# A recurrent attention layer with a gated feed-forward: loads and emission order rewritten, some steps moved to VectorE

## The chip, the cores and the metric

The kernel runs on one core of a Trainium2 chip. The metric is the device time of one execution in microseconds (us); of several executions the median is taken. A profile shows one execution: its span is the time from the first to the last instruction of the program. The engines are TensorE (PE, with its weight loads as PEld), VectorE (DVE), ScalarE (ACT), GpSimd (POOL) and SyncE (SP); SP issues most DMA transfers, POOL the weights' ones. Each engine works its own queue in order.

## The reference

Four sequences of 768 tokens, 8 heads of 48 channels. Per head a 48 x 48 state runs along the tokens:

```python
for t in range(S):
    cur = u * kt (outer) vt
    y[t] = rt @ (state + cur)
    state = wt * state + kt (outer) vt
```

The result, 3072 tokens of 384 channels, goes through a root-mean-square norm and a gated feed-forward of width 1536:

```python
xn  = x / sqrt(mean(x * x) + 1e-06) * rms_g
out = (silu(xn @ w_gate) * (xn @ w_val)) @ w_out
```

## The kernel before, in words

The tokens are cut into 24 chunks of 128, named n.j: n (0 to 5) is the place along the sequence, j (0 to 3) the sequence. Within a chunk the recurrence is written as matrix products. The steps of a chunk, each a small function of the program, are:

- load_w, load_r, load_k, load_v: DMAs on SP's queue, 192 KB each (384 KB for the w of n = 0 and 1, which are loaded together). The tiles rotate through 8 buffers each.
- ln and cs_mm: the logarithm of w (ScalarE) and its running sums on TensorE, in two PSUM banks (rings a and b, two banks each). For n = 0 and 1 both sums come from TensorE, later cs_add makes the second on VectorE. exp_r and exp_k (ScalarE) turn them into factors.
- r_mul, k_mul, w_tot: r and k times these factors, into bf16 tiles, and the decay of the chunk (VectorE; k_mul on POOL for the chunks listed in K_POOL).
- rk_pe and rk_tr: r and k transposed by TensorE and copied out of PSUM (n = 0 and 1), or transposed by a DMA (later).
- q_mm, q_mask_e, q_copy_o, q_mask_o: the products of r and k within the chunk, masked to the past.
- st_mm, st_new: the state after the chunk. cast_v: v in bf16.
- bonus_mul (POOL, two multiplications), bonus_sum (VectorE), bonus_v (POOL): the term with u.
- y_mm, x_add: the chunk's output x. x_sq, x_rstd, xn_mul: the norm; x_rstd takes two steps, on ScalarE for the chunks in RSTD_ACT, otherwise on POOL. xn_pe and xn_out (transposed by TensorE, copied out times the gain on VectorE), or xn_tr and xn_gain (by a DMA, and POOL) for n = 4 and 5.

Four chunks make a feed-forward group. Its 24 products of 512 columns, gate_mm.n.f and val_mm.n.f (f from 0 to 11, three matmuls each), use rings a and b too; silu (ScalarE) frees a bank of ring a and h_mul (VectorE) one of ring b. Then o_mm, o_out and out_dma give the output, 12 matmuls a chunk. The groups take chunks in order, except that chunks 0.0, 0.1, 1.0 and 1.1 make group 0 and 0.2, 0.3, 1.2 and 1.3 group 1. The weights of gate and val come in two parts: load_gv.0.x holds units 0 to 3, load_gv.1.x units 4 to 11 (x is 0 for gate, 1 for val). warm steps are matmuls of zeros whose result nobody reads.

What runs when is written out by hand: ORDER is a list of step names, and the program emits the steps in that order, so each engine's queue is the list with the other engines' steps taken out. All other PSUM tiles come from a ring of four banks, q. ScalarE holds one set of functions at a time: act (L234) emits a table load where a step needs the logarithm and exponential and the silu set is loaded, or the other way round.

Of the kernel before, what the change touches and what calls it, by code (L numbers as in the profile page):

```python
# [30 lines left out]
warm.1.0 warm.0.0 y_mm.0.1 load_k.1.1 load_r.1.1 load_k.0.3 load_v.0.3 q_mask_e.0.0 ln.0.3 w_tot.1.1 k_mul.1.0
r_mul.1.0 st_new.0.0 q_mask_o.0.0 w_tot.1.0 x_add.0.1 bonus_sum.0.0 rk_pe.1.0 rk_tr.1.0 k_mul.1.1 r_mul.1.1 st_mm.1.0
warm.4.0 cs_mm.0.3 x_sq.0.1 x_rstd.0.1 xn_mul.0.1 y_mm.0.0 bonus_v.0.0 q_mm.1.0 load_r.0.3 q_mask_e.1.0 x_add.0.0
q_mask_o.1.0 cs_mm.1.3 rk_pe.1.1 xn_pe.0.1 load_w.0.2 exp_k.0.3 warm.8.0 warm.7.0 warm.6.0 x_sq.0.0 exp_r.0.3
rk_tr.1.1 cast_v.0.3 ln.0.2 bonus_mul.1.1 k_mul.0.3 load_r.1.3 load_r.0.2 r_mul.0.3 xn_out.0.1 bonus_sum.1.0 warm.5.0
w_tot.0.3 st_new.1.0 bonus_sum.1.1 y_mm.1.0 rk_pe.0.3 rk_tr.0.3 x_rstd.0.0 bonus_v.1.0 st_mm.0.3 x_add.1.0 st_new.0.3
cs_mm.0.2 load_v.1.1 q_mm.0.3 warm.9.0 exp_r.0.2 q_copy_o.0.3 cast_v.1.1 xn_mul.0.0 exp_k.0.2 x_sq.1.0 load_v.0.2
x_rstd.1.0 exp_k.1.3 cast_v.0.2 xn_mul.1.0 exp_r.1.3 q_mm.1.1 q_mask_e.1.1 q_mask_o.1.1 r_mul.0.2 w_tot.0.2 load_k.0.2
bonus_v.1.1 load_gv.0.1 load_gv.0.0 warm.10.0 warm.11.0 st_mm.1.1 xn_pe.0.0 y_mm.1.1 st_new.1.1 x_add.1.1 cs_mm.1.2
x_sq.1.1 x_rstd.1.1 exp_r.1.2 q_mask_e.0.3 k_mul.0.2 st_mm.0.2 warm.14.0 warm.13.0 warm.12.0 xn_pe.1.0 load_k.1.3  # L40
load_gv.1.0 k_mul.1.3 q_mask_o.0.3 rk_pe.0.2 st_new.0.2 r_mul.1.3 xn_out.1.0 xn_out.0.0 xn_mul.1.1 load_r.1.2
load_k.1.2 load_v.1.3 bonus_mul.0.2 rk_pe.1.3 y_mm.0.3 xn_pe.1.1 xn_out.1.1 rk_tr.0.2 rk_tr.1.3 load_v.1.2 load_gv.1.1
q_mm.0.2 q_copy_o.0.2 warm.15.0 q_mm.1.3 load_w.2.1 load_w.2.0 q_mask_o.0.2 q_mask_e.0.2 w_tot.1.3 r_mul.1.2 exp_k.1.2
val_mm.0.1 val_mm.0.3 y_mm.0.2 bonus_sum.0.2 bonus_v.0.2 x_add.0.2 warm.19.0 q_copy_o.1.3 w_tot.1.2 q_mask_e.1.3
warm.18.0 warm.17.0 warm.16.0 gate_mm.0.3 gate_mm.0.1 q_mask_o.1.3 k_mul.1.2 x_sq.0.2 rk_pe.1.2 x_rstd.0.2 silu.0.3
silu.0.1 xn_mul.0.2 gate_mm.0.2 h_mul.0.3 warm.20.0 xn_pe.0.2 gate_mm.0.0 bonus_mul.1.2 bonus_mul.1.3 load_w.2.2
load_r.2.1 load_r.2.0 h_mul.0.1 silu.0.2 rk_tr.1.2 load_w.2.3 val_mm.0.2 val_mm.0.0 h_mul.0.2 bonus_sum.1.2
bonus_sum.1.3 bonus_mul.0.3 gate_mm.0.9 silu.0.9 silu.0.0 h_mul.0.0 bonus_sum.0.3 q_mm.1.2 gate_mm.0.6 silu.0.6
gate_mm.0.5 silu.0.5 q_copy_o.1.2 q_mask_e.1.2 load_wo.0.0 load_wo.2.0 bonus_v.0.3 gate_mm.0.7 gate_mm.0.4 load_wo.1.0
q_mask_o.1.2 bonus_v.1.3 bonus_v.1.2 val_mm.0.9 cast_v.1.3 x_add.0.3 xn_out.0.2 val_mm.0.5 x_sq.0.3 cast_v.1.2  # L50
h_mul.0.9 y_mm.1.3 h_mul.0.5 y_mm.1.2 x_add.1.3 load_k.2.1 x_add.1.2 silu.0.4 silu.0.7 val_mm.0.4 gate_mm.0.8 x_sq.1.3
x_rstd.0.3 x_sq.1.2 h_mul.0.4 x_rstd.1.3 silu.0.8 xn_mul.0.3 xn_mul.1.3 val_mm.0.8 val_mm.0.6 h_mul.0.8 h_mul.0.6
x_rstd.1.2 gate_mm.0.10 st_mm.1.2 st_new.1.2 gate_mm.0.11 xn_mul.1.2 xn_pe.1.3 xn_pe.1.2 val_mm.0.10 xn_pe.0.3
st_mm.1.3 silu.0.10 silu.0.11 load_r.2.2 h_mul.0.10 ln.2.1 val_mm.0.7 val_mm.0.11 xn_out.0.3 xn_out.1.2 h_mul.0.11
h_mul.0.7 cs_mm.2.1 load_k.2.0 load_r.2.3 ln.2.0 cs_mm.2.0 cs_add.2.1 exp_r.2.1 cs_add.2.0 xn_out.1.3 exp_r.2.0
exp_k.2.1 ln.2.2 w_tot.2.1 r_mul.2.1 o_mm.0.0 w_tot.2.0 k_mul.2.1 bonus_mul.2.1 ln.2.3 exp_k.2.0 r_mul.2.0 o_out.0.0
o_mm.0.1 cs_mm.2.2 cs_mm.2.3 cs_add.2.2 o_out.0.1 exp_r.2.2 w_tot.2.2 cs_add.2.3 exp_k.2.2 exp_k.2.3 exp_r.2.3
load_v.2.1 r_mul.2.2 w_tot.2.3 r_mul.2.3 load_k.2.3 o_mm.0.2 val_mm.1.6 gate_mm.1.6 k_mul.2.0 silu.1.6 val_mm.1.0
cast_v.2.1 gate_mm.1.0 st_mm.2.1 gate_mm.1.1 bonus_mul.2.0 o_out.0.2 h_mul.1.6 bonus_sum.2.1 silu.1.0 silu.1.1
val_mm.1.1 gate_mm.1.5 load_k.2.2 bonus_v.2.1 bonus_mul.2.3 k_mul.2.2 k_mul.2.3 out_dma.0.1 load_v.2.0 gate_mm.1.4  # L60
h_mul.1.0 st_new.2.1 st_new.1.3 h_mul.1.1 o_mm.0.3 silu.1.5 gate_mm.1.7 val_mm.1.4 rk_tr.2.1 rk_tr.2.0 bonus_sum.2.0
bonus_sum.2.3 o_out.0.3 q_mm.2.0 silu.1.4 h_mul.1.4 q_mask_e.2.1 silu.1.7 q_copy_o.2.1 gate_mm.1.3 val_mm.1.7
q_mask_e.2.0 q_copy_o.2.0 cast_v.2.0 load_v.2.3 load_v.2.2 load_w.3.1 out_dma.0.0 load_r.3.2 cast_v.2.2 rk_tr.2.3
rk_tr.2.2 out_dma.0.2 load_w.3.0 st_mm.2.0 st_mm.2.2 q_mask_o.2.1 val_mm.1.3 q_mask_o.2.0 bonus_v.2.0 load_v.3.2
load_w.3.3 y_mm.2.1 gate_mm.1.2 load_r.3.3 load_k.3.2 load_k.3.0 h_mul.1.7 y_mm.2.0 silu.1.3 silu.1.2 val_mm.1.5
gate_mm.1.8 load_w.3.2 load_r.3.0 load_r.3.1 gate_mm.1.9 bonus_mul.2.2 cast_v.2.3 st_new.2.2 st_new.2.0 x_add.2.0
x_add.2.1 q_mm.2.2 x_sq.2.0 h_mul.1.5 h_mul.1.3 val_mm.1.9 q_mask_e.2.2 bonus_sum.2.2 x_sq.2.1 silu.1.8 val_mm.1.2
load_k.3.1 gate_mm.1.11 q_copy_o.2.3 silu.1.9 x_rstd.2.1 x_rstd.2.0 h_mul.1.9 st_mm.2.3 gate_mm.1.10 q_copy_o.2.2
xn_mul.2.0 xn_mul.2.1 silu.1.11 bonus_v.2.2 q_mask_o.2.2 q_mask_o.2.3 bonus_v.2.3 xn_pe.2.0 val_mm.1.8 y_mm.2.2
h_mul.1.2 load_k.3.3 st_new.2.3 q_mask_e.2.3 silu.1.10 ln.3.0 xn_pe.2.1 val_mm.1.10 y_mm.2.3 h_mul.1.8 ln.3.1  # L70
val_mm.1.11 cs_mm.3.0 cs_mm.3.1 x_add.2.2 x_sq.2.2 h_mul.1.10 x_add.2.3 ln.3.3 x_sq.2.3 x_rstd.2.2 h_mul.1.11
xn_mul.2.2 o_mm.1.0 cs_add.3.1 xn_out.2.0 cs_add.3.0 o_out.1.0 exp_r.3.1 exp_r.3.0 xn_pe.2.2 o_mm.1.1 exp_k.3.0 ln.3.2
x_rstd.2.3 xn_mul.2.3 exp_k.3.1 k_mul.3.0 load_k.4.1 w_tot.3.0 w_tot.3.1 out_dma.0.3 load_v.3.1 out_dma.1.0 r_mul.3.0
r_mul.3.1 cast_v.3.2 cs_mm.3.2 xn_out.2.2 k_mul.3.1 cs_add.3.2 cs_mm.3.3 xn_pe.2.3 exp_k.3.2 cs_add.3.3 exp_r.3.3
o_out.1.1 rk_tr.3.0 k_mul.3.2 o_mm.1.2 xn_out.2.3 r_mul.3.3 st_mm.3.2 o_out.1.2 exp_k.3.3 w_tot.3.3 exp_r.3.2 o_mm.1.3
k_mul.3.3 rk_tr.3.1 o_out.1.3 load_v.3.0 load_v.3.3 w_tot.3.2 xn_out.2.1 st_new.3.2 r_mul.3.2 val_mm.2.5 q_mm.3.0
q_copy_o.3.0 gate_mm.2.0 q_mask_e.3.0 bonus_mul.3.0 gate_mm.2.5 cast_v.3.0 st_mm.3.0 val_mm.2.0 q_mask_o.3.0
cast_v.3.1 bonus_sum.3.0 q_mask_e.3.1 cast_v.3.3 bonus_v.3.0 st_mm.3.1 y_mm.3.0 silu.2.0 h_mul.2.0 load_k.5.3
bonus_mul.3.3 bonus_mul.3.1 silu.2.5 load_k.5.2 out_dma.1.2 x_add.3.0 h_mul.2.5 gate_mm.2.7 gate_mm.2.1 st_new.3.1
x_sq.3.0 silu.2.1 silu.2.7 val_mm.2.6 val_mm.2.1 gate_mm.2.6 h_mul.2.1 gate_mm.2.3 val_mm.2.7 load_w.4.1 rk_tr.3.2  # L80
rk_tr.3.3 load_k.4.0 load_k.4.3 load_r.4.2 load_w.4.0 load_v.4.0 load_r.4.1 out_dma.1.3 load_r.5.0 q_copy_o.3.1
load_r.4.3 load_r.4.0 st_new.3.0 silu.2.6 h_mul.2.6 gate_mm.2.2 x_rstd.3.0 q_mask_o.3.1 q_mm.3.2 bonus_sum.3.1
h_mul.2.7 val_mm.2.2 q_mask_e.3.3 q_mask_e.3.2 bonus_mul.3.2 silu.2.2 q_copy_o.3.2 gate_mm.2.4 val_mm.2.3 st_mm.3.3
bonus_v.3.1 y_mm.3.1 xn_mul.3.0 xn_pe.3.0 silu.2.4 silu.2.3 load_k.4.2 q_mask_o.3.2 gate_mm.2.11 h_mul.2.3 gate_mm.2.8
# [604 lines left out]
```

## Time and profile before

| | |
|---|---|
| time, median of 3 runs | 212.51 us |
| lowest and highest run | 207.11 and 213.64 us |
| span of the profiled execution | 202.6 us |
| time of the profiled execution itself | not given by its profile |
| busy: PE, DVE, ACT, POOL | 190.6, 146.2, 137.0, 135.1 us |
| DMA | 32.41 MB, mean 160 GB/s |
| first feed-forward product | 34.40 us after the start |

Line numbers such as L602 are those of the kernel before. In a row of a group stand the line, the engine, the operation, what it writes and reads, the shapes and the count; after the bar the busy time, the mean time of one in ns, and the idle time of the engine ahead of these instructions with what ended it. In a row in order of time the first two numbers are the start and the duration in us.

### The profile page before, as it was taken

To read this page: it belongs to the slowest core of one execution; us is meant where nothing else is said; L and a number is where in the kernel's file an instruction comes from. 1 tells how busy PE (TensorE), PEld (TensorE's weight loads), DVE (VectorE), ACT (ScalarE), POOL (GpSimd) and SP (SyncE) were. 2 spreads that over 40 slices of the span, in tenths; PEclk is the share of its full clock that TensorE was granted. 3 is DMA by queue.
4 is the path that set the end of the run, shared out by engine and by line. 5 is a ranking of instruction groups with operands and counts; after the bars stand their busy time and mean duration, and the time that the engine had idled before them with its cause. 6 is when DMAs were issued, how large, how long until landed. Compare 5 with 4: busy or idle time off the path is not lost.

```text
span 202.6 us, 4390 instructions
## 1 busy us (share of the span) xinstructions
PE 190.6 (94%) x1573; PEld 112.8 (56%) x1573; DVE 146.2 (72%) x289; ACT 137.0 (68%) x278; POOL 135.1 (67%) x198
## 2 busy tenths in 40 slices
PE   1998887899999999999999999999999999999994
...
DVE  6489787458786989998779889878688782075411
...
GB/s 165 232 235 168 245 177 206 203 191 192 217 191 220 195 148 190 209 216 197 220 173 221 231 188 228 186 199 131 38 135 123 52 22 80 57 0 42 39 134 101
DMA packets 121566, 32.41 MB, mean 160 GB/s; under 512 B 116420, under 2 KB 120392, under 8 KB 121544
## 3 DMA queue, kind: packets, MB, share of 16 engines
...
q14 instruction: 10, 0.08, 0.1%
...
## 4 chain that ended last, share of the span: by engine, by line
PE 59%; SPq 11%; DMA 9%; DVE 6%; POOL 5%; ACT 5%; issue 3%; DVEq 0%; POOLq 0%
PE ps_au L602 9%; SPq L249 9%; PE ps_bu L602 8%; PE ps_bv L602 8%; PE ps_av L602 8%; PE ps_qx L634 6%; PE ps_qv L634 5%; DMA rt<-in_r_dram 4%; PE ps_qu L634 3%; PE ps_qz L634 2%; DMA wt<-in_w_dram 2%; DMA vt<-in_v_dram 2%; DMA out_dram<-ob 2%; POOL ruk L457 1%; SPq L262 1%
## 5 line engine op out<-in xcount | busy, mean ns | idle before, releaser
L634 PEld LDWEIGHTS <-ht 128*128 128x128 bf16 x300 | 28.5, 98 | 17.3
L620 DVE TENSOR_TENSOR ht<-ps_bu,sg 128x512 bf16<-128x512 f32 x38 | 26.1, 687 | 14.5 <-PE ps_bu L602 9.8
L602 PEld LDWEIGHTS <-wg_sb 128*128 128x128 bf16 x216 | 23.2, 114 | 19.1 <-issue 0.6
L602 PEld LDWEIGHTS <-wv_sb 128*128 128x128 bf16 x216 | 22.9, 114 | 18.2
L236 ACT ACTIVATE sg<-ps_au 128x512 bf16<-128x512 f32 x38 | 22.6, 595 | 14.7 <-PE ps_au L602 13.8
L620 DVE TENSOR_TENSOR ht<-ps_bv,sg 128x512 bf16<-128x512 f32 x34 | 23.3, 686 | 12.7 <-ACT sg L236 6.4
L602 PE MATMUL ps_au<-xnt,wg_sb 128*128 128x512 bf16 x114 | 30.9, 380 | 0.4 <-ACT sg L236 0.4
L602 PE MATMUL ps_bu<-xnt,wv_sb 128*128 128x512 bf16 x114 | 30.9, 380 | 0.0
L236 ACT ACTIVATE sg<-ps_av 128x512 bf16<-128x512 f32 x34 | 20.2, 595 | 14.0 <-PE ps_av L602 12.9
L602 PE MATMUL ps_bv<-xnt,wv_sb 128*128 128x512 bf16 x102 | 27.6, 380 | 0.0
L602 PE MATMUL ps_av<-xnt,wg_sb 128*128 128x512 bf16 x102 | 27.6, 380 | 0.0
L457 POOL TENSOR_TENSOR ruk<-rt,kt 128x384 f32<-128x384 f32 x24 | 24.3, 1013 | 4.2 <-DMA kt<-in_k_dram 4.2
L451 POOL TENSOR_TENSOR rk<-kt,ek 128x384 bf16<-128x384 f32 x20 | 19.9, 1002 | 9.0 <-ACT ek L236 9.0
L458 POOL TENSOR_TENSOR ruk<-ruk,u_bc 128x384 f32<-128x384 f32 x24 | 24.0, 999 | 1.9
L467 POOL TENSOR_TENSOR ydiag<-vt,diag 128x384 f32<-128x384 f32 x24 | 20.1, 841 | 7.5 <-DVE diag L462 5.1
L550 ACT ACTIVATE junk<-xb 128x384 bf16<-128x384 f32 x24 | 12.5, 520 | 5.2 <-DVE xb L545 5.0
L634 PE MATMUL ps_qx<-wo_sb,ht 128*128 128x384 bf16 (+1 forms) x96 | 15.9, 316 | 0.0
L563 ACT ACTIVATE xn<-xb,rstd 128x384 bf16<-128x384 f32 x24 | 14.3, 610 | 0.7 <-POOL rstd L559 0.6
L510 POOL TENSOR_SCALAR_AFFINE_SELECT qts<-qts 128x512 bf16<-128x512 bf16 x20 | 12.5, 636 | 3.1 <-ACT qts L503 3.1
L234 ACT ACT_TABLE_LOAD x10 | 12.8, 1283 | 1.8 <-PEq L673 1.7
L462 DVE TENSOR_REDUCE diag<-ruk 128x8 f32<-128x384 f32 x24 | 12.9, 543 | 0.0
L634 PE MATMUL ps_qv<-wo_sb,ht 128*128 128x384 bf16 x72 | 12.7, 326 | 0.0
...
## 6 DMA issues: line engine op xcount, KB each, us to landing
...
wt<-in_w_dram SPq DMA_DIRECT2D x4, 384.0 KB, 4.3
wo_sb<-in_moe_w_out_dram POOLq DMA_DIRECT2D x3, 384.0 KB, 7.3
wg_sb<-in_moe_w_gate_dram POOLq DMA_DIRECT2D x1, 768.0 KB, 10.0
```

Of the source, the lines that this page charges most:

```text
L234: nc.scalar.preload_act_table_set(table_name)
L236: return nc.scalar.activation(**kw).ins
L249: dmas["load_" + which, n, j] = nc.sync.dma_start(out=inp[which, n, j], in_=t[j, :, n * L:(n + 1) * L, :].rearrange("h t d -> t h d")).ins
L451: eng.tensor_tensor(out=rk[:, n % 2, j, 1, :, 0:D], in0=inp["k", n, j], in1=bank["cs_k", n, j][:, 0:DM].rearrange("p (h d) -> p h d", h=H) ...
L457: nc.gpsimd.tensor_tensor(out=ruk[n, j], in0=inp["r", n, j], in1=inp["k", n, j], op=ALU.mult)
L458: nc.gpsimd.tensor_tensor(out=ruk[n, j], in0=ruk[n, j], in1=u_bc, op=ALU.mult)
L462: nc.vector.tensor_reduce(out=diag[n, j].rearrange("p h o -> p (h o)"), in_=ruk[n, j], axis=mybir.AxisListType.X, op=ALU.add)
L467: nc.gpsimd.tensor_tensor(out=ydiag[n, j], in0=inp["v", n, j], in1=diag[n, j].to_broadcast([128, H, D]), op=ALU.mult)
L563: nc.scalar.activation(out=xn, in_=xb[n, j], func=AF.Copy, scale=rstd[n, j][:, 1:2])
L602: nc.tensor.matmul(ps, lhsT=units(ws, c, f), rhs=xnt[n].rearrange("p (c x) -> p c x", c=KC)[:, c, :], start=(c == 0), stop=(c == KC - 1))
L620: nc.vector.tensor_tensor(out=ht[n][:, f, :], in0=bank.pop(("v", n, f)), in1=bank.pop(("sg", n, f)), op=ALU.mult)
L634: nc.tensor.matmul(ps[:, cols], lhsT=ht[n][:, f, b * L:(b + 1) * L], rhs=wo_sb[:, f, cols], start=(f == 0), stop=(f == FC - 1))
```

## The change

ORDER is replaced by another list of the same steps. In it the r and k of chunks 0.0, 1.0, 0.1 and 1.1 are loaded first behind the two w tiles, then v; load_gv.0.1 and load_gv.0.0 stand among the first group's attention steps; the attention of 0.2, 0.3, 1.2 and 1.3 stands mostly behind the first feed-forward products; six warm steps stand ahead of the first cs_mm and five behind the last o_mm.

The lists that give a step to an engine change as well: some casts of v and products of x with 1/rms go to VectorE, as do five copies of the transposed r and k, nine of POOL's k_mul and, the other way, five copies of outputs go from VectorE to ScalarE; x_rstd goes to ScalarE for eight more chunks.

```diff
-load_w.0.1 load_w.0.0 load_v.0.1 ln.0.1 load_r.0.1 load_k.0.1 load_k.0.0 load_r.0.0 cs_mm.0.1 ln.0.0 exp_k.0.1
...
+warm.6.0 load_w.0.0 ln.0.0 warm.15.0 load_w.0.1 warm.2.0 warm.18.0 load_r.0.0 load_k.0.0 load_k.1.0 warm.0.0 warm.13.0
+load_k.0.1 bonus_mul.0.0 load_r.1.0 ln.0.1 load_r.0.1 cs_mm.0.0 bonus_mul.0.1 exp_r.0.0 load_r.1.1 load_k.1.1
...
+exp_k.0.2 xn_out.1.0 xn_out.1.1 gate_mm.0.2 bonus_mul.0.3 exp_r.0.2 load_k.0.2 w_tot.0.2 load_v.0.3 rk_tr.0.3 q_mm.0.3
...
-    CAST_ACT = sel("00 01 02 03 10 11 12 13")
+    CAST_ACT = sel("00 10 11 20 50")
     EXPR_SB = sel("")
-    K_POOL = sel("02 03 12 13 20 21 22 23 30 31 32 33 40 41 42 43 50 51 52 53")
-    EXPK_SB = sel("10 11") | K_POOL
+    XN_DVE = sel("00 01 02 03 10 12 13 22 30 32 41 42 51 52 53")
+    CAST_DVE = sel("12 13 22 23 30 40 41 42 43 51 52")
+    K_POOL = sel("03 13 20 21 23 30 32 40 41 43 51")
+    EXPK_SB = sel("02 03 10 11 12 13 20 21 22 23 30 31 32 33 40 41 42 43 50 51 52 53")
...
-    RK_DVE = sel("")
+    RK_DVE = sel("00 02 03 10 13")
     ODD_DVE = sel("00 01 10 11")
-    RSTD_ACT = sel("00 01 10 11")
-    OUT_DVE = sel("00 02 10 12 20 22 30 32 40 42 50 52 53")
+    RSTD_ACT = sel("00 02 10 11 13 21 33 43 50 51 52 53")
+    OUT_DVE = sel("01 10 22 32 41 42 52 53")
...
         if (n, j) in CAST_ACT:
             nc.scalar.copy(out=vb[n, j], in_=inp["v", n, j])
+        elif (n, j) in CAST_DVE:
+            nc.vector.tensor_copy(out=vb[n, j], in_=inp["v", n, j])
         else:
             nc.gpsimd.tensor_copy(out=vb[n, j], in_=inp["v", n, j])
...
-        nc.scalar.activation(out=xn, in_=xb[n, j], func=AF.Copy, scale=rstd[n, j][:, 1:2])
+        if (n, j) in XN_DVE:
+            nc.vector.tensor_scalar(out=xn, in0=xb[n, j], scalar1=rstd[n, j][:, 1:2], scalar2=None, op0=ALU.mult)
+        else:
+            nc.scalar.activation(out=xn, in_=xb[n, j], func=AF.Copy, scale=rstd[n, j][:, 1:2])
```

200 lines of the change are left out of this document (99 added, 101 removed).

## The prediction

> **What bounds the kernel now.** I read the page's busy shares, its slices and its chain first, then the table by stretches of time.
>
> ```profile
> span 202.6 us, 4390 instructions
> PE 190.6 (94%) x1573; PEld 112.8 (56%) x1573; DVE 146.2 (72%) x289; ACT 137.0 (68%) x278; POOL 135.1 (67%) x198
> PE   1998887899999999999999999999999999999994
> DVE  6489787458786989998779889878688782075411
> PE 59%; SPq 11%; DMA 9%; DVE 6%; POOL 5%; ACT 5%; issue 3%; DVEq 0%; POOLq 0%
> ```
>
> ```profile
> 20.00:30.00 10.00, 8.47 (x97) 5.25 (x95) 8.08 (x19) 9.71 (x25) 7.62 (x9) 0.84 1.11 212
> 60.00:70.00 10.00, 10.00 (x65) 5.77 (x64) 7.32 (x16) 6.01 (x11) 8.65 (x10) 1.00 0.91 198
> 80.00:90.00 10.00, 10.00 (x103) 6.52 (x101) 9.57 (x21) 9.06 (x21) 6.49 (x11) 1.00 1.04 219
> ```
>
> There are two regimes. From about 40 us TensorE is full: 10.00 of 10 us, even where VectorE is busy 9.57 (columns: PE, PEld, DVE, ACT, POOL, clock, DMA share). Before that it is not (8.47 at a clock of 0.84 from 20 to 30 us): the first feed-forward product waits for four chunks (0.0, 0.1, 1.0, 1.1) to go through attention. So time changes in two ways only: the first product starts earlier or later, with more or less work left behind it, or another engine takes the bound later.
>
> **The start, now.** TensorE's and VectorE's order of time:
>
> ```profile
> 5.95 0.82 PE L396 MATMUL ps_au<-lw,mw 128*128 128x384 bf16 x2
> 11.88 0.34 PE L520 MATMUL ps_qz<-vb,rk 128*128 128x96 bf16 x4
> 12.06 0.49 PE L396 MATMUL ps_av<-lw,mw 128*128 128x384 bf16 x2
> 16.71 0.49 PE L396 MATMUL ps_av<-lw,mw 128*128 128x384 bf16 x2
> 17.57 0.36 PE L540 MATMUL ps_qx<-vb,qts 128*128 128x48 bf16 x8
> 21.52 0.33 PE L537 MATMUL ps_qu<-st,rkT 128*128 128x96 bf16 x4
> 21.93 0.61 PE L474 MATMUL ps_qx<-ident,rk 128*128 128x128 bf16 x8
> 22.38 0.33 PE L520 MATMUL ps_qv<-vb,rk 128*128 128x96 bf16 x4
> 34.40 0.84 PE L602 MATMUL ps_bu<-xnt,wv_sb 128*128 128x512 bf16 x3
> 36.81 0.70 PE L374 MATMUL ps_qx<-zero 128*128 128x384 bf16 x2 [0.72 <-DVE xb L545]
> ```
>
> ```profile
> 8.40 0.55 DVE L451 TENSOR_TENSOR rk<-kt,ps_bu 128x384 bf16<-128x384 f32 x1 [1.95 <-DMA kt<-in_k_dram]
> 14.12 0.85 DVE L451 TENSOR_TENSOR rk<-kt,ek 128x384 bf16<-128x384 f32 x1
> 17.42 0.54 DVE L451 TENSOR_TENSOR rk<-kt,ek 128x384 bf16<-128x384 f32 x1
> 17.89 0.54 DVE L445 TENSOR_TENSOR rk<-rt,ps_au 128x384 bf16<-128x384 f32 x1
> 18.35 0.68 DVE L499 TENSOR_TENSOR qts<-ps_qu,mask_lt 128x512 bf16<-128x512 f32 x1
> 18.95 0.54 DVE L545 TENSOR_TENSOR xb<-ps_qx,ydiag 128x384 f32<-128x384 f32 x1
> 32.37 0.56 DVE L588 TENSOR_TENSOR xnt<-ps_qx,gT 128x384 bf16<-128x384 bf16 x1 [0.42 <-PE ps_qx L578]
> 14.51 1.32 POOL L457 TENSOR_TENSOR ruk<-rt,kt 128x384 f32<-128x384 f32 x1
> ```
>
> The first product is at 34.40. From start to start a 384-wide VectorE step costs 0.47 (17.42 to 17.89), a 512-wide one 0.60 (18.35 to 18.95). Priced so, VectorE's queue up to the last of the four xn_out is 20.7 us of work, done between 8.40 and 32.93, so it worked 84% of that stretch.
>
> **The start, changed.** Fewer steps stand ahead of the first product. TensorE's queue loses 2 cs_mm (16.71 to 17.57: 0.86), 2 rk_pe (21.93 to 22.38: 0.45), 1 y_mm (21.52 to 21.93: 0.41), and 3 q_mm, 3 st_mm and 2 warm-ups, which I put at 0.2 each (11.88 to 12.06: 0.18): 1.7 + 0.9 + 0.4 + 1.6 = 4.6 us, which must be done later. Five warm-ups go behind the last outputs, where nothing waits for them, so 1.0 falls away: net 3.6.
>
> When does it start? Six warm-ups now precede the first cs_mm, which began at 5.95; at the slow pace of that moment (0.82 for two overlapping) they take about 0.3 each, so cs_mm.0.0 starts near 7.8 and the first k_mul near 10 instead of 8.40. VectorE then has, up to xn_out.1.1: 4 k_mul, 5 r_mul, 4 bonus_sum, 4 x_add, 4 xn_out, 2 st_new (23 x 0.47 = 10.8), 8 masks (4.8), 5 w_tot (0.08 each by their spacing, 0.4), and, new, 2 rk_tr and 3 xn_mul. No row shows these two. For rk_tr, a 1024-wide copy out of PSUM, the bounds are 0.55 (a 384-wide step) and 1.25 (the 1.07 ns per element between the 384- and 512-wide rows, times 640, on top of 0.55); I take 1.1, near ScalarE's 1.01 for the same copy (next fence). For xn_mul and the casts they are 0.27 (half the 384-wide row) and 0.54; I take 0.40. Sum 19.4. At 90% working (the first group's data are loaded first, so less waiting than the 84% of now) the first product comes at 10 + 19.4/0.90 = 31.5. Bounds: 17.9 us at 95% gives 28.9; 20.1 at 84% gives 33.9.
>
> The weights must be there too:
>
> ```profile
> 26.57 0.78 POOL L351 DMA_DIRECT2D wg_sb<-in_moe_w_gate_dram  x1
> 28.32 0.80 POOL L351 DMA_DIRECT2D wg_sb<-in_moe_w_gate_dram  x1
> wg_sb<-in_moe_w_gate_dram POOLq DMA_DIRECT2D x1, 384.0 KB, 7.4
> wv_sb<-in_moe_w_val_dram POOLq DMA_DIRECT2D x1, 384.0 KB, 5.2
> wg_sb<-in_moe_w_gate_dram POOLq DMA_DIRECT2D x1, 768.0 KB, 10.0
> ```
>
> In the new order load_gv.0.0 stands on POOL behind bonus_v.1.0, which needs bonus_sum.1.0, two thirds down VectorE's list: near 24, so it lands at 29 to 32. It is no earlier bound than VectorE. load_gv.1.0 stands behind x_rstd.0.1 and k_mul.0.3: issued near 27.5, landed near 37.5, and gate_mm.0.9, the seventh product, wants it near 31.5 + 6 x 0.65 = 35.4. I price that stall at 1.5 (0 to 3). It takes the place of a like one now: the 0.72 at 36.81 and shorter ones up to 44.
>
> Start: 31.5 - 34.4 + 3.6 = **+0.7**, weights against old stalls **0**.
>
> **The steady part.** Rows for what changes hands:
>
> ```profile
> 49.62 0.65 PE ps_av L602 x3
> 56.50 1.97 PE ps_qu L634 x12
> L563 ACT ACTIVATE xn<-xb,rstd 128x384 bf16<-128x384 f32 x24 | 14.3, 610 | 0.7 <-POOL rstd L559 0.6
> L381 POOL CAST vb<-vt 128x384 bf16<-128x384 f32 x16 | 7.9, 506 | 0.4 <-DMA vt<-in_v_dram 0.4
> L483 ACT COPY rkT<-ps_qu 128x1024 bf16<-128x1024 bf16 x4 | 4.0, 1012 | 0.2 <-PE ps_qu L474 0.2
> L451 POOL TENSOR_TENSOR rk<-kt,ek 128x384 bf16<-128x384 f32 x20 | 19.9, 1002 | 9.0 <-ACT ek L236 9.0
> L234 ACT ACT_TABLE_LOAD x10 | 12.8, 1283 | 1.8 <-PEq L673 1.7
> ```
>
> - POOL gives up 9 k_mul (1.0 each), 8 casts (0.5) and 8 x_rstd: some 19 of 135 us. It is not the bound now, so I count this as nothing.
> - ScalarE gives up 15 xn_mul (0.61), 5 rk_tr and 3 casts, and takes 5 o_out (0.5) and 8 x_rstd. Its emitted order needs 16 table loads instead of 10: 6 x 1.28 = 7.7 us. Two of the three extra pairs lie inside the feed-forward groups 0 and 1, where silu stops for 3.4 to 4.2 us. Behind each, TensorE has 3 to 4 us of cs_mm, st_mm, y_mm and products that need no new silu, so I take 0.5 for both; uncovered they would cost up to 3.5.
> - VectorE takes 9 k_mul (0.47), 15 xn_mul and 11 casts (0.40), 5 rk_tr (1.1), less 5 o_out: 4.2 + 10.4 + 5.5 - 2.4 = +17.7 us. The work in its queue from the first product of group 0 to that of group 1 is 12 h_mul and 4 masks at 0.60 (9.6), 24 steps at 0.47 (11.3), 5 st_new (0.5, and twice that for the three that add the old state: 4.0), 5 w_tot (0.4), 3 rk_tr (3.3), 6 casts and xn_mul (2.4): 31.0 us. TensorE's in the same stretch is 24 products at 0.65 (15.6), 4 outputs at 1.95 (7.8) and 7.8 of attention steps priced as above: 31.2. Now that ratio is 19.8 to 25.8, and at most 26.8 to 30.2 (group 1). Counted from the first product to the last xn_out of groups 1, 2 and 3, the new queue stands at 31, 57 and 83 us against TensorE's 31, 57 and 85. So VectorE runs level with TensorE and any wait of its own becomes TensorE's. I charge **+2.0** (0 to 6).
>
> Sum: 0.7 + 0.5 + 2.0 = +3.2: span 205.8. The tail after the last output keeps its length, a copy and a store of half a tile as now. The page gives no time of the profiled execution beside its span; the three timed runs are 4.5 to 11.0 above 202.6. On the median of 212.51 the same difference gives **215.7 us**, 1.5% slower. About 2% is what the timing of this kernel tells from no change.
>
> [...] The trace shows one k_mul with both inputs in SBUF at 0.85 while POOL was computing, and one at 0.54 that started while POOL was idle; the POOL step that began beside the first took 1.32 instead of 1.0. [...]
>
> **Rivals.**
> - *VectorE becomes the bound* (slower). It collides with POOL: 15 + 11 + 9 = 35 new operations of the kind of the 14.12 row, 0.31 dearer each, 10.9 us in all, of which some 17, or 5.3 us, fall before the last xn_out of group 3, where the margin is 2. With a twentieth of idling (4 us) the lag there is 83 + 5 + 4 - 85 = 7 us. Price +7 instead of +2: about 220.7. It decides once VectorE's queue passes TensorE's at that point. For: the level sums. Against: 9.57 of 10 cost TensorE nothing at 80 to 90 us, and POOL has less to do. Chance 0.28.
> - *The start is really shorter* (faster). Copies at their lower bounds and little waiting put the first product at 28.9 and leave VectorE 4 us of margin: -5.5 + 3.6 = -1.9, no steady loss, and 1.5 of old stalls gone: about 209.1; if the six warm-ups also cost less than the 1.6 I gave them, 207.5. For: first loads are the first needed. Against: the weights' landing. Chance 0.24.
> - *The weights come late*: gate_mm.0.9 and val_mm.0.9 wait 3 us and more: about 218. Chance 0.10.
> - That the change does nothing cannot be: every queue is reordered.
>
> **How the numbers follow.** The forecast, 212.5 to 218, has 0.38. The range 206 to 222 takes in all but the ends of the rivals. Faster by over 2% (below 208.3) is the better half of the second rival: 0.13. Slower by over 2% (above 216.8) is the first and third rival, less their mild cases, and the upper third of the forecast: 0.45. Within 2%: 0.42.
>
> **What would show it.** The first L602 row near 31.5 with 12 to 13 us of TensorE work before it; VectorE's work without long idling from 10 us on; L234 x16; in the stretches from 35 to 100 us VectorE at 9 or more of 10 and, if I am right, TensorE losing 2 us there, ended by ht or xnt. VectorE rows for xn and vb under 0.35 would speak for the second rival, rows over 0.6 beside POOL for the first. I am wrong if the first product comes before 29 or after 34, or if clear TensorE gaps follow silu at the two added table pairs.

## The result, and the profile after

The changed kernel takes **212.0 us** (median of 4 runs, 211.27 to 212.58); the kernel before, run beside it, 210.02 (207.11 to 213.64). The ratio is **1.0256**, 95% interval 1.0204 to 1.0308: slower. The ratio leaves out executions that ran slow, most of them of the kernel before, and is therefore not the quotient of the two medians. The forecast was 215.7 us, 1.5% slower.

The profiled execution took 212.13 us, with a span of 210.4. From its page (all line numbers of the changed kernel are 2 to 7 higher than before: L609 is the gate and value product, L641 the output product):

```profile
span 210.4 us, 4375 instructions
...
PE 190.9 (91%) x1553; PEld 112.1 (53%) x1573; DVE 164.3 (78%) x324; ACT 136.9 (65%) x282; POOL 120.2 (57%) x165
...
PE   2975878999899999998999889998989999999995
...
DVE  5289989499997899999699999979966997144511
...
PE 42%; DVE 13%; POOL 11%; SPq 9%; issue 9%; DMA 7%; ACT 6%; POOLq 1%; DVEq 0%; ACTq 0%
...
L236 ACT ACT_TABLE_LOAD x16 | 20.5, 1283 | 1.9 <-PEq L680 1.6
```

TensorE is busy as long as before, 190.9 us, in a span that is 7.8 longer. (These 7.8 us lie between the two profiled executions. The ratio stands for some 5.3 us: what lies outside the span was 1.7 us in every later run, so the profiled execution of before took about 204.3, less than any of the four timed beside the changed kernel.) VectorE has 35 instructions and 18.1 us more, and the chain that ended last runs through VectorE for 13% and GpSimd for 11%, where it was 6% and 5%. In the table by stretches (columns: PE, PEld, DVE, ACT, POOL, clock, DMA share), first the kernel before, then the changed one:

```profile
90.00:100.00 10.00, 10.00 (x86) 5.80 (x84) 8.33 (x18) 6.88 (x14) 8.93 (x13) 1.00 1.07 207
...
120.00:130.00 10.00, 10.00 (x83) 5.75 (x80) 9.18 (x19) 6.67 (x14) 9.82 (x13) 1.00 0.99 215
```

```profile
80.00:90.00 10.00, 9.95 (x108) 6.14 (x108) 9.93 (x21) 9.90 (x23) 3.58 (x7) 1.00 0.92 189
90.00:100.00 10.00, 9.17 (x75) 5.40 (x76) 9.72 (x21) 7.60 (x18) 9.12 (x12) 1.00 0.76 174
...
120.00:130.00 10.00, 8.58 (x65) 4.93 (x65) 9.92 (x23) 6.50 (x16) 7.87 (x8) 1.00 0.97 182
```

In the changed kernel VectorE is at 9.7 to 9.9 of 10, and TensorE, which before was at 10.00 in all three stretches, loses 0.8 and 1.4 us in the second and third. TensorE's order of time shows where (start, duration; in brackets the wait and who ended it):

```profile
7.85 0.85 PE L400 MATMUL ps_au<-lw,mw 128*128 128x384 bf16 x2
...
31.70 0.84 PE L609 MATMUL ps_au<-xnt,wg_sb 128*128 128x512 bf16 x2 [1.07 <-DMA wg_sb<-in_moe_w_gate_dram]
...
37.05 0.84 PE L609 MATMUL ps_av<-xnt,wg_sb 128*128 128x512 bf16 x3 [0.82 <-DMA wg_sb<-in_moe_w_gate_dram]
...
57.60 0.65 PE L641 MATMUL ps_qz<-wo_sb,ht 128*128 128x384 bf16 x3 [0.70 <-DMA wo_sb<-in_moe_w_out_dram]
...
96.39 0.84 PE L609 MATMUL ps_av<-xnt,wg_sb 128*128 128x512 bf16 x2 [0.68 <-DVE wcol L445]
...
121.70 0.33 PE L524 MATMUL ps_qz<-vb,rk 128*128 128x96 bf16 x4 [1.23 <-DVE xnt L595]
...
146.31 0.81 PE L609 MATMUL ps_bv<-xnt,wv_sb 128*128 128x512 bf16 x3 [0.91 <-DVE ht L627]
...
156.81 0.81 PE L609 MATMUL ps_au<-xnt,wg_sb 128*128 128x512 bf16 x2 [0.85 <-POOL xnt L600]
```

The first product starts 2.7 us earlier (31.70 for 34.40). Behind it I add up TensorE's waits: the time from one start to the next, less what the first one's columns take where TensorE runs on at a clock of 1.00 (0.16 us for 384 columns, 0.65 for three times 512), where more than 0.25 us is left. These six and four shorter ones come to 7.3 us; before it was three waits and 1.7. What TensorE does behind its first product, waits taken off, went from 163.3 to 168.4 us. That is the balance of the last TensorE start (207.46 for 199.41): -2.7 for the start, +5.1 for work moved behind it (0.8 of it the five warm-ups behind the last output), +5.6 for waits, 8.0 in all; the tail behind that start is 0.3 shorter.

At 96, 121 and 146 us TensorE waits for VectorE, and in all three places VectorE has just done one or two of its **new** steps, slowly. VectorE, then GpSimd, in order of time:

```profile
93.05 1.35 DVE L455 TENSOR_TENSOR rk<-kt,ek 128x384 bf16<-128x384 f32 x1
...
119.21 0.82 DVE L568 TENSOR_SCALAR xn<-xb,rstd 128x384 bf16<-128x384 f32 x1
119.96 1.15 DVE L383 CAST vb<-vt 128x384 bf16<-128x384 f32 x1
...
121.11 0.54 DVE L595 TENSOR_TENSOR xnt<-ps_qz,gT 128x384 bf16<-128x384 bf16 x1
...
143.95 0.81 DVE L383 CAST vb<-vt 128x384 bf16<-128x384 f32 x1
144.68 0.98 DVE L568 TENSOR_SCALAR xn<-xb,rstd 128x384 bf16<-128x384 f32 x1
145.58 0.68 DVE L627 TENSOR_TENSOR ht<-ps_bv,sg 128x512 bf16<-128x512 f32 x1
```

```profile
92.88 1.11 POOL L461 TENSOR_TENSOR ruk<-rt,kt 128x384 f32<-128x384 f32 x1
...
118.82 1.00 POOL L455 TENSOR_TENSOR rk<-kt,ek 128x384 bf16<-128x384 f32 x1 [0.19 <-ACT ek L238]
119.78 1.11 POOL L461 TENSOR_TENSOR ruk<-rt,kt 128x384 f32<-128x384 f32 x1
...
143.32 1.23 POOL L514 TENSOR_SCALAR_AFFINE_SELECT qts<-qts 128x512 bf16<-128x512 bf16 x2
144.51 0.93 POOL L471 TENSOR_TENSOR ydiag<-vt,diag 128x384 f32<-128x384 f32 x1
```

With GpSimd idle the same steps take 0.55 (k_mul with its factor in SBUF), 0.42 (product with 1/rms) and 0.35 (cast): so 0.80, 0.40 + 0.80 and 0.46 + 0.56 us are stretch, and TensorE's whole gaps at the three places, counted as above, are 0.84, 1.39 and 1.07. Steps with an operand in PSUM (L595, L627) took 0.54 to 0.56 and 0.67 to 0.69 in this trace, with a GpSimd step beside them or without, and bonus_sum, a sum over one SBUF tile, 0.54 to 0.55 in all 24.

The rows also say how long a stretch is. At the three places the stretched step ends 0.21 to 0.41 us after the end of the GpSimd step that was running when it began. The k_mul ends 0.41 behind GpSimd's product (92.88 + 1.11 = 93.99, against 94.40). The product and the cast at the second place end 0.21 and 0.22 behind theirs, and the cast and the product at the third 0.21 and 0.22 behind the masks and the bonus of v. Of the 21 casts, xn products and k_mul in this trace that began while a computing step of GpSimd had 0.15 us or more to go, 20 end so: 0.41 to 0.42 us behind it for a k_mul, 0.21 to 0.22 for the others. (The other one, an xn product of 0.41 at 26.13, ran beside GpSimd's step on one column, L563.) In these 20 it is as if VectorE's step stood still until GpSimd's is through.

### The profile page after: what moved, and what is told of

Read it like the earlier page. It is cut to its first block, busy times and chain, and to the rows that moved or that the text cites. A ratio compares the mean times of both kernels' runs of the same rounds, so it can differ in the third digit from the quotient of the medians.

```text
span 210.4 us, 4375 instructions
## 1 busy us (share of the span) xinstructions
PE 190.9 (91%) x1553; PEld 112.1 (53%) x1573; DVE 164.3 (78%) x324; ACT 136.9 (65%) x282; POOL 120.2 (57%) x165
## 4 chain that ended last, share of the span: by engine, by line
PE 42%; DVE 13%; POOL 11%; SPq 9%; issue 9%; DMA 7%; ACT 6%; POOLq 1%; DVEq 0%; ACTq 0%
PE ps_au L609 7%; PE ps_av L609 7%; PE ps_bu L609 6%; SPq L251 6%; PE ps_bv L609 5%; DMA wo_sb<-in_moe_w_out_dram 3%; PE ps_qz L641 3%; SPq L264 2%; POOL xnt L600 2%; PE ps_qx L641 2%; PE ps_qv L641 2%; DVE rk L449 2%; DMA rt<-in_r_dram 2%; ACT junk L554 2%; DVE rk L455 1%
## 5 line engine op out<-in xcount | busy, mean ns | idle before, releaser
L641 PEld LDWEIGHTS <-ht 128*128 128x128 bf16 x300 | 27.8, 98 | 18.0 <-DVE ht L627 1.1
L609 PEld LDWEIGHTS <-wg_sb 128*128 128x128 bf16 x216 | 23.1, 114 | 24.4 <-DMA wg_sb<-in_moe_w_gate_dram 2.5
L627 DVE TENSOR_TENSOR ht<-ps_bv,sg 128x512 bf16<-128x512 f32 x37 | 25.2, 682 | 12.9 <-PE ps_bv L609 6.7
L609 PEld LDWEIGHTS <-wv_sb 128*128 128x128 bf16 x216 | 23.1, 114 | 20.1 <-issue 1.4
L627 DVE TENSOR_TENSOR ht<-ps_bu,sg 128x512 bf16<-128x512 f32 x35 | 24.0, 685 | 12.2 <-ACT sg L238 7.2
L609 PE MATMUL ps_au<-xnt,wg_sb 128*128 128x512 bf16 x109 | 30.6, 381 | 2.2 <-DMA wg_sb<-in_moe_w_gate_dram 1.1
L609 PE MATMUL ps_bv<-xnt,wv_sb 128*128 128x512 bf16 x104 | 29.5, 380 | 1.6 <-DVE ht L627 0.9
L461 POOL TENSOR_TENSOR ruk<-rt,kt 128x384 f32<-128x384 f32 x24 | 25.2, 1048 | 7.3 <-DMA kt<-in_k_dram 3.6
L609 PE MATMUL ps_av<-xnt,wg_sb 128*128 128x512 bf16 x99 | 27.5, 380 | 1.8 <-DMA wg_sb<-in_moe_w_gate_dram 0.8
L609 PE MATMUL ps_bu<-xnt,wv_sb 128*128 128x512 bf16 x100 | 27.7, 380 | 0.1
L641 PE MATMUL ps_qz<-wo_sb,ht 128*128 128x384 bf16 (+1 forms) x120 | 20.4, 318 | 0.7 <-DMA wo_sb<-in_moe_w_out_dram 0.7
L641 PE MATMUL ps_qx<-wo_sb,ht 128*128 128x384 bf16 x84 | 15.0, 326 | 0.1
L455 POOL TENSOR_TENSOR rk<-kt,ek 128x384 bf16<-128x384 f32 x11 | 10.9, 1000 | 6.6 <-ACT ek L238 6.5
L238 ACT ACTIVATE lw<-wt 128x384 bf16<-128x384 f32 (+1 forms) x20 | 11.4, 578 | 2.1 <-DMA wt<-in_w_dram 2.1
```

Source lines behind the costliest of these rows:

```text
L238: return nc.scalar.activation(**kw).ins
L455: eng.tensor_tensor(out=rk[:, n % 2, j, 1, :, 0:D], in0=inp["k", n, j], in1=bank["cs_k", n, j][:, 0:DM].rearrange("p (h d) -> p h d", h=H) ...
L461: nc.gpsimd.tensor_tensor(out=ruk[n, j], in0=inp["r", n, j], in1=inp["k", n, j], op=ALU.mult)
L609: nc.tensor.matmul(ps, lhsT=units(ws, c, f), rhs=xnt[n].rearrange("p (c x) -> p c x", c=KC)[:, c, :], start=(c == 0), stop=(c == KC - 1))
L627: nc.vector.tensor_tensor(out=ht[n][:, f, :], in0=bank.pop(("v", n, f)), in1=bank.pop(("sg", n, f)), op=ALU.mult)
L641: nc.tensor.matmul(ps[:, cols], lhsT=ht[n][:, f, b * L:(b + 1) * L], rhs=wo_sb[:, f, cols], start=(f == 0), stop=(f == FC - 1))
```

## The experiments

Two theories of where the lost time comes from stood at the beginning: **A**, the new lists, that is VectorE's added work and its stretching beside GpSimd; **B**, the new order. Later theory **C** took A's place: not the sum of VectorE's work, but a stretched step ahead of one that TensorE needs (D is its rival, as each expectation words it). All kernels are the changed kernel with the edit named; ratios are to the kernel before on the same chip.

**The order without the lists, and the lists without the order.** In the first kernel the lists are set back, in the second ORDER is:

```diff
-    CAST_ACT = sel("00 10 11 20 50")
+    CAST_ACT = sel("00 01 02 03 10 11 12 13")
-    XN_DVE = sel("00 01 02 03 10 12 13 22 30 32 41 42 51 52 53")
-    CAST_DVE = sel("12 13 22 23 30 40 41 42 43 51 52")
+    XN_DVE = sel("")
+    CAST_DVE = sel("")
...
```

> The new order with every step on the engine it had before: VectorE loses 15 xn_mul, 11 casts, 9 k_mul and 5 rk_tr (26 us with their waits for POOL), ScalarE and POOL get them back. Theory A (VectorE, level with TensorE and waiting for POOL, makes the loss after the start): the gaps at 96, 121 and 146 us go, ratio to the kernel before 0.99 to 1.005, though the start may be 1 us later because ScalarE's copy of rkT takes 1.0 instead of 0.69. Theory B (the order itself makes the loss): ratio 1.02 to 1.04.

> The old order with the new lists of engines. Theory A: VectorE gets 17 us more and some 8 us of waits for POOL in a queue that had 10 us of margin at group 3, ratio 1.01 to 1.03, TensorE gaps ended by VectorE after 60 us. Theory B: ratio 0.99 to 1.005.

Measured: order alone 228.88 us, **1.1038** (1.0847 to 1.1229); lists alone 236.94 us, **1.1519** (1.1439 to 1.16). Both expectations missed by far. Either half by itself costs four to six times what the whole does. The longest wait of TensorE with the order alone is for GpSimd's gain, which itself had waited 2.32 us for the DMA that transposes x; the second fence shows what GpSimd did ahead of an earlier wait of 2.7 us, at 166.88:

```profile
199.89 0.81 PE L609 MATMUL ps_au<-xnt,wg_sb 128*128 128x512 bf16 x2 [4.21 <-POOL xnt L600]
```

```profile
163.09 2.96 POOL L455 TENSOR_TENSOR rk<-kt,ek 128x384 bf16<-128x384 f32 x3
166.00 0.83 POOL L600 TENSOR_TENSOR xnt<-xnt,gT 128x384 bf16<-128x384 bf16 x1
```

Three k_mul stand there on GpSimd ahead of the gain that group 4's first product needs; the changed kernel has one there. With the lists alone TensorE's longest wait hangs on ScalarE:

```profile
199.71 1.10 PE L641 MATMUL ps_qv<-wo_sb,ht 128*128 128x384 bf16 x2 [5.24 <-DVE ht L627]
```

```profile
192.78 1.28 ACT L236 ACT_TABLE_LOAD   x1
...
195.19 1.28 ACT L236 ACT_TABLE_LOAD   x1
...
197.03 1.28 ACT L236 ACT_TABLE_LOAD   x1
198.33 0.60 ACT L238 ACTIVATE sg<-ps_au 128x512 bf16<-128x512 f32 x1
```

The x_rstd that the new list gives to ScalarE fall between two silu in the old order, and each costs a pair of table loads; there are 20 loads in all. So the question "the order or the lists" has no answer: each in-order queue is laid out for one list, and the change is one thing.

**The weights earlier.** load_gv and load_wo are moved up in GpSimd's order; in the second kernel the logarithm of chunk 0.2 and its sums are also moved down:

```diff
-... bonus_sum.0.0 bonus_mul.1.0 ... cast_v.0.1 q_mm.1.0 q_mask_e.1.0 load_gv.0.1 ... x_add.0.1 load_gv.0.0 ...
+... bonus_sum.0.0 load_gv.0.0 load_gv.0.1 bonus_mul.1.0 ... bonus_v.0.1 load_gv.1.0 ... bonus_v.1.0 load_gv.1.1 ...
 second kernel:
-... bonus_v.1.0 st_new.0.0 cast_v.1.1 ln.0.2 ... load_r.0.2 cs_mm.0.2 ...
+... x_rstd.1.1 ln.0.2 ... xn_pe.1.1 cs_mm.0.2 ...
```

> The changed kernel with the seven weight loads issued earlier on POOL (both first parts ahead of bonus_mul.1.0, the second parts behind bonus_v.0.1 and bonus_v.1.0, w_out behind cast_v.0.2). In the changed kernel TensorE waits 1.24 for the first weights, 0.99 for the second, 0.87 for w_out. If the weights' places cost what these gaps say: first product near 30.5 instead of 31.7 and 2 to 3 us faster than the changed kernel (ratio 1.01 to 1.015). If VectorE's queue is the bound behind them: the gaps go and come back as waits for VectorE, under 1 us faster (ratio 1.02 to 1.026).

> As the kernel with early weights (gate and value weights issued 6 us earlier, output weights earlier too), but the gates' logarithm of chunk 0.2 stands behind the four x_rstd on ScalarE, and its cumulative sum behind the four xn_pe on TensorE. Theory: in the first kernel with early weights the first product came 1.8 us later only because the weights' packets held up the load of w of chunk 0.2, for which ScalarE waited 3.99 us with the squares of x queued behind it. Then the first product now comes at 29.5 to 31 us without a wait for weights, the waits at 37.05 and 57.60 (1.9 us) are gone, and the time is 1.5 to 3 us below the changed kernel's on this chip. Rival: the transfers share one capacity, and the loads of chunks 0.2 and 0.3 are as late as before; TensorE then waits in the first feed-forward group instead, and the time is the changed kernel's or above.

Measured: 214.9 us, **1.0437** (1.0329 to 1.0546), and 213.82 us, **1.0329** (1.0256 to 1.0402). The waits for weights are gone in both, and the first product comes later, at 33.54 and 32.97. In the first kernel ScalarE's order of time shows why:

```profile
25.18 0.84 ACT L238 ACTIVATE lw<-wt 128x768 bf16<-128x768 f32 x1 [3.99 <-DMA wt<-in_w_dram]
```

With the first weights issued near 15 us instead of 21 to 24, ScalarE waited 3.99 us for the w of chunk 0.2 instead of 0.31, its logarithm began at 25.18 instead of 21.91, and the squares of x queue behind it. In the second kernel that wait is gone, but TensorE has little to do (2.81 of 5 us from 25 to 30), and its rows are slow:

```profile
28.51 0.50 PE L585 MATMUL ps_qv<-ident,xn 128*128 128x128 bf16 x3 [2.19 <-DVE xn L568]
...
32.97 1.49 PE L609 MATMUL ps_au<-xnt,wg_sb 128*128 128x512 bf16 x3
```

Three transposes take 0.50 where they take 0.33 otherwise, three products 1.49 where they take 0.84: the granted clock was 0.50 to 0.57 from 20 to 35 us. (In the changed kernel it was 0.53 from 20 to 25 us, then 0.78, and 1.00 from 30 us on.) The 2 us of waiting for gate weights could not be had back in this way.

**k_mul back on GpSimd.**

```diff
-    K_POOL = sel("03 13 20 21 23 30 32 40 41 43 51")
+    K_POOL = sel("02 03 12 13 20 21 22 23 30 31 32 33 40 41 42 43 50 51 52 53")
```

> The changed kernel with the nine k_mul back on POOL. VectorE loses 9 x 0.91 = 8 us, POOL gets 9. Theory A: 2 to 3 us faster than the changed kernel (ratio 1.01 to 1.015), and the gaps ended by VectorE shrink by half. Theory B, or if another VectorE step makes the waits: ratio 1.02 to 1.03.

Measured: 214.52 us, **1.0409** (1.0301 to 1.0518). The wait at 96 us, where the stretched k_mul was, is gone, and that at 146 fell from 1.07 to 0.57; but GpSimd now has two k_mul ahead of the gain for group 4:

```profile
158.31 0.81 PE L609 MATMUL ps_au<-xnt,wg_sb 128*128 128x512 bf16 x2 [2.24 <-POOL xnt L600]
```

```profile
155.52 1.95 POOL L455 TENSOR_TENSOR rk<-kt,ek 128x384 bf16<-128x384 f32 x2 [0.34 <-ACT ek L238]
157.43 0.82 POOL L600 TENSOR_TENSOR xnt<-xnt,gT 128x384 bf16<-128x384 bf16 x1
```

A wait was taken away at VectorE and made at GpSimd.

**The changed kernel once more, as a yardstick.**

> The changed kernel once more, as the yardstick for the three kernels run beside it. Every theory expects the ratio of the first comparison, 1.02 to 1.035, a span of 210 to 212 us, the first feed-forward product at 31.5 to 32 us, and some 6 to 7.5 us of waits of over 0.25 us in TensorE's queue behind it. If the ratio lies near 1.04, the 1.041 and 1.044 of the two earlier one-part kernels were nothing but another chip.

Measured: 211.77 us, **1.0239** (1.0182 to 1.0296), span 210.1, first product at 31.23, waits behind it 7.1 us with the same three places (0.84, 1.39, 1.07).

**The six warm-ups.**

```diff
-warm.6.0 load_w.0.0 ln.0.0 warm.15.0 load_w.0.1 warm.2.0 warm.18.0 load_r.0.0 load_k.0.0 load_k.1.0 warm.0.0 warm.13.0
+load_w.0.0 ln.0.0 load_w.0.1 load_r.0.0 load_k.0.0 load_k.1.0
...
+warm.6.0 warm.15.0 warm.2.0 warm.18.0 warm.0.0 warm.13.0   (behind the last output)
```

> The changed kernel with the six warm-ups ahead of the first cumulative sum moved behind the last outputs. Theory of the prediction, that they cost the start their own time: the first cumulative sum at 5.9 instead of 7.85, the first k_mul near 8.4 instead of 10.10, xnt ready near 29.5; the first product gains no more than the weights allow (landed 31.65), so 0 to 1.5 us less than the changed kernel on this chip. Rival, that they earn their time by the granted clock: the clock falls earlier than at 20 us, the attention steps up to the first product take longer, and the time is 0 to 2 us more.

Measured: 210.55 us, **1.0177** (1.011 to 1.0244), 1.2 less than the yardstick beside it; the intervals overlap. The first k_mul starts at 8.16, and the weights, there by 28.84, do not hold the first product as I had thought; its last wait is for VectorE's xn_out:

```profile
28.84 0.81 PE L609 MATMUL ps_au<-xnt,wg_sb 128*128 128x512 bf16 x3 [0.67 <-DVE xnt L595]
```

That is 2.4 us earlier than in the yardstick; the profiled span is 2.1 shorter, the median 1.2. The clock did not fall earlier: it was 1.00 from 10 to 20 us in both.

**Less work on GpSimd.** First the second multiplication of bonus_mul is left out (24 steps of 1.0 us), then both:

```diff
 first:
-        nc.gpsimd.tensor_tensor(out=ruk[n, j], in0=ruk[n, j], in1=u_bc, op=ALU.mult)
 second:
-        nc.gpsimd.tensor_tensor(out=ruk[n, j], in0=inp["r", n, j], in1=inp["k", n, j], op=ALU.mult)
-        nc.gpsimd.tensor_tensor(out=ruk[n, j], in0=ruk[n, j], in1=u_bc, op=ALU.mult)
...
-        nc.vector.tensor_reduce(..., in_=ruk[n, j], ...)
+        nc.vector.tensor_reduce(..., in_=u_bc, ...)
```

> The changed kernel without the second of GpSimd's two multiplications in each bonus_mul (by u): 24 steps of 1.0 us less on GpSimd, so the output lacks u; VectorE, ScalarE and TensorE keep every step. Theory A, that VectorE's new steps are stretched by GpSimd working beside them and VectorE's lag becomes TensorE's waits: the stretched rows of xn, vb and k_mul get fewer, VectorE's busy time falls by 2 to 4 us from 164.3, the waits at 96, 122, 129 and 146 us (3.6 us in all) at least halve, ratio 1.005 to 1.015. Theory B, that the waits come from where the steps stand in the queues, whatever GpSimd does: the waits stay within 0.5 us of what they are, ratio as the changed kernel's on this chip within 0.005.

> The changed kernel without bonus_mul: GpSimd's 48 multiplications are left out and the sum on VectorE, with its length kept, reads the row of u instead, so the output lacks the product of r and k in the bonus term. VectorE keeps every step and its order. Theory C by place: at 93 us the k_mul of 1.35 us had these multiplications beside it, so it falls to 0.55 and the wait of 0.84 behind it goes; at 119 us the cast of 1.15 had one beside it and the xn product of 0.82 GpSimd's k_mul, so the wait of 1.39 loses some 0.8; at 144 us the cast and the product had a mask and the bonus of v beside them, so the wait of 1.07 stays. Theory D, that the order alone makes these waits, however long the steps: all three stay within 0.2.

Measured for the first: 210.89 us, **1.0181** (1.0092 to 1.027). 24 us less work on GpSimd brought 0.9 us beside the yardstick, and the three waits stand at 0.84, 1.39 and 1.06. By its expectation that speaks for B; but the stretched steps at these places were as long as before (VectorE's busy time fell by 0.7 us only), because the GpSimd steps running when they began were not the ones left out: the first multiplication or a k_mul at the first two places, a mask and the bonus of v at the third. So this run had not taken away what it meant to take away.

Measured for the second: 207.81 us, **1.0134** (1.0102 to 1.0165), on the chip of the next kernels. VectorE has the same steps in the same order:

```profile
91.71 0.54 DVE L455 TENSOR_TENSOR rk<-kt,ek 128x384 bf16<-128x384 f32 x1
...
117.06 0.83 DVE L566 TENSOR_SCALAR xn<-xb,rstd 128x384 bf16<-128x384 f32 x1
117.81 0.34 DVE L383 CAST vb<-vt 128x384 bf16<-128x384 f32 x1
...
140.48 0.80 DVE L383 CAST vb<-vt 128x384 bf16<-128x384 f32 x1
141.20 0.98 DVE L566 TENSOR_SCALAR xn<-xb,rstd 128x384 bf16<-128x384 f32 x1
```

```profile
118.75 0.33 PE L522 MATMUL ps_qz<-vb,rk 128*128 128x96 bf16 x4 [0.43 <-DVE xnt L593]
```

The k_mul fell from 1.35 to 0.54 and its wait is gone. The cast fell from 1.15 to 0.34, the product beside GpSimd's k_mul stayed at 0.83, and the gap went from 1.39 to 0.59. (GpSimd's two k_mul stand at 116.67 to 117.67 and from 117.93, and the cast fits between them.) At the third place both steps and the gap (1.06) stayed. That is theory C's forecast, place by place, and it excludes the rival of this run, that the order makes these waits however long the steps: at each place the gap fell by as much as the steps ahead of it. The profiled span is 3.6 us shorter than the yardstick's: 0.9 because the first product comes earlier, 2.4 in waits, of which 1.6 at the first two places. The changed kernel itself was not run on this chip, so the times give the size less surely than the rows. What is left of the loss here, 1.3%, fits the work moved behind the first product and the remaining 4.7 us of waits; that part was not tried by itself.

**The stretched steps put behind the awaited ones**, five steps at the three places:

```diff
-... xn_mul.2.2 k_mul.3.1 exp_r.3.3 ... w_tot.3.2 r_mul.3.2 ...
+... xn_mul.2.2 exp_r.3.3 ... w_tot.3.2 r_mul.3.2 k_mul.3.1 ...
-... xn_mul.3.2 o_mm.2.0 load_r.4.0 exp_r.4.1 cast_v.4.3 ... xn_out.3.0 ... xn_out.3.1 ...
+... o_mm.2.0 load_r.4.0 exp_r.4.1 ... xn_out.3.0 ... xn_out.3.1 xn_mul.3.2 cast_v.4.3 ...
-... cast_v.4.2 gate_mm.3.10 ... xn_mul.4.1 ... h_mul.3.11 ...
+... gate_mm.3.10 ... h_mul.3.11 xn_mul.4.1 cast_v.4.2 ...
```

> The changed kernel with five VectorE steps moved behind the step that TensorE waits for at three places, nothing else: k_mul.3.1 behind r_mul.3.2 (the wait at 96 us, 0.84), cast_v.4.3 and xn_mul.3.2 behind xn_out.3.1 (121 us, 1.39), cast_v.4.2 and xn_mul.4.1 behind h_mul.3.11 (146 us, 1.07). Theory C, that a new VectorE step, stretched by GpSimd's work beside it, stands in VectorE's order ahead of the step that TensorE needs: the three waits go and the span falls by 2.3 to 3.3 us, ratio 1.008 to 1.014 where the changed kernel again had 1.024. Theory D, that VectorE as a whole is behind: the waits come back at the next step that TensorE needs from VectorE, and the gain is under 1 us.

Measured: 213.16 us, **1.0354** (1.025 to 1.0457): no gain. The three waits are gone, and one of 2.04 us has come at 124.29 (with a smaller one, of 0.57, at 147.91). VectorE, TensorE and the stretches of time around it:

```profile
120.54 1.09 DVE L568 TENSOR_SCALAR xn<-xb,rstd 128x384 bf16<-128x384 f32 x1
121.55 1.15 DVE L383 CAST vb<-vt 128x384 bf16<-128x384 f32 x1
122.70 1.07 DVE L383 CAST vb<-vt 128x384 bf16<-128x384 f32 x1
123.69 0.54 DVE L449 TENSOR_TENSOR rk<-rt,ps_au 128x384 bf16<-128x384 f32 x1
```

```profile
124.29 0.46 PE L415 MATMUL ps_au<-lw,mask_lt 128*128 128x384 bf16 x1 [1.91 <-DVE rk L449]
```

```profile
122.00:124.00 2.00, 0.39 (x6) 0.23 (x4) 2.00 (x4) 0.19 (x1) 1.92 (x3) 1.00 0.75 145
124.00:126.00 2.00, 1.71 (x14) 1.10 (x15) 1.97 (x6) 0.19 (x1) 0.63 (x1) 0.59 1.01 242
126.00:128.00 2.00, 2.00 (x8) 0.95 (x7) 1.96 (x6) 1.98 (x6) 1.62 (x2) 0.55 1.24 160
```

Three stretched steps now stand in a row ahead of the next thing that TensorE needs, r_mul.4.0; their stretch (0.67 + 0.80 + 0.72) is as long as the wait. That is the rival's forecast of this run: the stretch makes the wait, but with VectorE at 9.9 of 10 this place for 2 us of it was no more harmless than the old ones. Other places were not tried. And here the wait cost more than itself, since TensorE's clock was 0.59 and 0.55 in the 4 us behind it, which by an estimate (the lost shares of these two stretches) is another 1.7 us.

**All mends together**: the moves that the expectation lists, with the gain of group 4 on VectorE, and then with one weights' load earlier:

```diff
-    GAIN_POOL = (4, 5)
+    GAIN_POOL = (5,)
 second kernel, too:
-... x_rstd.0.1 ... xn_out.0.0 load_gv.1.0 ...
+... load_gv.1.0 x_rstd.0.1 ... xn_out.0.0 ...
```

> The moves of the three places, the six warm-ups behind the last outputs, the output weights' loads issued as soon as GpSimd is through cast_v.0.2 (7 us earlier), and the gains of group 4 on VectorE instead of GpSimd. If the waits of the changed kernel are separate costs: 1.3 (warm-ups) + 3.3 (three places) + 0.9 (output weights) + 0.5 (half of the wait at 157) = 6.0 us less than the changed kernel, so a span of 204 to 205.5 and a ratio of 0.993 to 1.003. If VectorE or the attention work behind the first product sets the time, less than half of it: above 1.010.

> As the kernel with all mends, and the second part of the gate weights issued ahead of x_rstd.0.1 on GpSimd, some 2 us earlier. If its landing alone makes gate_mm.0.9 wait (1.0 to 1.3 us): 1 us less than the kernel with all mends. If the transfers share one capacity, the loads of chunk 0.2 come later by as much, and the time is the same or more.

Measured: 212.42 us, **1.0334** (1.0245 to 1.0423), and 211.23 us, **1.0255** (1.0167 to 1.0342). The waits were not separate costs: of the 6.0 us nothing came. In the second kernel the wait for weights at 37 us is gone, and one of 2.2 us for GpSimd's k_mul stands at 51 us. None of the kernels with all of the work beats the kernel before.

## Why the prediction was right or wrong

The time came out within the range and 1.7% below the number; but two errors of opposite sign lie in that, so its closeness is luck. That the kernel gets slower was right.

- **First k_mul and first product: right.** The warm-ups were to put the first cs_mm at 7.8 and the first k_mul near 10; measured 7.85 and 10.10, and 8.16 without them. The first product was to come at 31.5 and came at 31.70. Two terms of the sum were off and cancelled: the rk_tr copies took 0.68, not 1.1, and one of the first k_mul took 1.37, not 0.47. So the right start is luck in part. The gate weights ended the last wait before it, 0.4 us after VectorE's last xn_out (through at 31.25): I had held the weights to be no bound, and they lay as close as that.
- **Work moved behind it: right, a little low.** I had 4.6 us moved, of which five warm-ups were not to count (net 3.6); measured 5.1 more work behind the first product, those warm-ups (0.8) among it (net 4.3).
- **Weights: right in kind.** gate_mm.0.9 waited 0.99 (I had 1.5, 0 to 3). I did not follow load_wo, which GpSimd issues late because bonus_v waits 7.6 us for VectorE's sum ahead of it: 0.87 at 57 us.
- **Table loads: right in number, 0.5 too dear.** There were 16, and of TensorE's waits of over 0.25 us none was for a silu.
- **VectorE level with TensorE: the step that failed in size.** I charged 2.0 (0 to 6) and looked for them from 35 to 100 us. TensorE's waits ended by VectorE add up to 4.1, of which 3.3 at the three places, and only 1.1 lie before 100 us. The sum of the queue was about right (17.7 priced, 18.1 more busy time measured), but by luck in part: alone, from start to next start, a cast takes 0.27, an xn_mul 0.33 and an rk_tr 0.60, where I had 0.40, 0.40 and 1.1, and the stretch made up for it. What I left to the first rival was that the new steps are stretched to a mean of 0.53, 0.57 and 0.91 (casts, xn_mul, k_mul with its factor in SBUF). That GpSimd's work makes this stretch is what the run without bonus products shows (1.35 to 0.54 and 1.15 to 0.34); the rival's price of +7 was too high: by these means the stretch is 11 x 0.18 + 15 x 0.15 + 11 x 0.36 = 8.2 us (for two of the k_mul it is not new), and most of it falls where nobody waits.
- **GpSimd is not the bound, so counted as nothing: wrong at one place.** Its gain for group 4 made TensorE wait 1.01 us at 156.81.
- **From span to time: wrong.** Span +3.2 was predicted and +7.8 measured. I then put the sum on a median of 212.51, taking the profiled execution for a typical one. What lies outside the span was 1.7 us in every later run, so the profiled execution of before took about 204.3 and lies below each of the timed runs that I had. The sum was 4.6 too small (3.1 of it waits: 5.6 more were measured, 2.5 stood in the sum) and the base some 8 too high.
- **Which new steps are stretched: right in kind, too dear.** The first rival counted all 35 as steps of the kind of the k_mul at 14.12, 0.31 dearer each. For the casts and xn_mul no row of the kernel before shows that; it was my estimate. The changed kernel's rows show a stretch for all three kinds, of 0.18, 0.15 and 0.36 us in the mean (casts, xn_mul, k_mul with its factor in SBUF), and not for the rows with an operand in PSUM (0.54 to 0.56 and 0.67 to 0.69).
